# A new order of the work ahead of the MLP: scalings off GpSimd, a token tile loaded ahead of the weight transposes

## The chip, the cores and the metric

The kernel runs on one core of a Trainium2 chip. The metric is the device time of one execution in microseconds; the median of three runs stands for a kernel. The engines are TensorE (PE), VectorE (DVE), ScalarE (ACT), GpSimd (POOL) and SyncE (SP), which here only issues DMAs.

## What is computed

One transformer block over 2048 tokens of width 576, in bfloat16:

```python
def _A_ref(x, wqkv, w_phi, wo):          # 32 heads of 18
    qkv = (x @ wqkv) -> q, k, v per head
    pq, pk = q @ w_phi, k @ w_phi        # per head, 18 x 18
    phi_q = concat(softmax(pq), softmax(-pq)); phi_k = likewise
    kv = sum over tokens of phi_k^T v;  z = sum over tokens of phi_k
    o = (phi_q @ kv) / (phi_q @ z + 1e-6)
    return o @ wo
def _B_ref(x, w1, b1, w2, b2):           # hidden width 4608
    return gelu(layernorm(x) @ w1 + b1) @ w2 + b2
h  = x + _A_ref(layernorm(x), ...)
h2 = h + _B_ref(layernorm(h), ...)
```

The sums over tokens (kv, z) run over all keys, so no query can be finished until every key has been through; then the MLP follows, tile by tile.

## The kernel before

The 2048 tokens are 16 tiles of 128, handled as 8 pairs `p` with halves. The program has two parts. The first takes all keys and values, and the queries' feature maps, and ends with the first token pair normalised for the MLP. The second is the MLP and what is left of the attention output, in blocks of one or two pairs (`first_block` to `double_block`), and it keeps TensorE busy to the end.

The order in the first part is written out by hand: a flat list of calls, lines 772 to 1103. All five engines are under manual scheduling, so each engine executes its own instructions in the order in which the calls issue them, and each DMA queue likewise. A call whose operands are not ready holds up everything behind it on the same engine. The calls:

- `load_x` loads tokens, `load_values` the value weights, `turn_wk` and `turn_wq` transpose the key and query weights from DRAM (three DMA transposes each, on SP's queue); `load_phi` loads w_phi on ScalarE's queue.
- `spread(g)` (GpSimd) lays w_phi out in blocks; `fold_k_mm`/`fold_k_ev` multiply it into the key weights, nine products with a copy out of PSUM each; `fold_mm("q", c)`/`fold_ev` do the same to the query weights in five, and `swap_q` copies parts of them to the other half of the partitions by DMA.
- `stats(p, i)` (VectorE) and `power` (GpSimd's pow) give mean and reciprocal deviation. `scale(p, i, engine)` normalises one tile: a tensor_scalar on VectorE or GpSimd, or an activation on ScalarE, for which `centre` (GpSimd) prepares the shift.
- Pairs 0 and 1 are transposed on TensorE (`turn_x_mm`, `turn_x_ev`), pairs 2 to 7 by DMA (`turn_dma`), which waits for both scaled halves.
- `key_mm`, `value_mm`, `query_mm` are projections, 18 matmuls each. `key_exp`, `query_exp` write two exponentials of each to a buffer, `key_sum`, `query_sum` (VectorE) sum over each head and take reciprocals, `key_weigh`, `query_weigh` multiply by them, on VectorE or GpSimd.
- `sums(p, a)` adds one tile's keys and values up in PSUM; `window_masks` (GpSimd) makes the mask that `table` (VectorE) applies to the finished sums. Then `turn_q`, `combine_mm`, `divide`, `turn_o_mm`, the residual and the second normalisation follow, and `turn2_mm` hands the first tile to the MLP.

Projections, folds and transposes share one PSUM pool, `two`, of three buffers: a fourth waits for the copy or exponential that empties the first. The exponentials of the keys have five buffers for eight pairs. `filler(n)` issues n small matmuls that compute nothing that is used.

Of the kernel before, what the change touches and what calls it, by code (L numbers as in the profile page):

```python
# [45 lines left out]
def kernel(  # L46
# [148 lines left out]
    load_x(1, 2, nc.scalar)  # L195
# [586 lines left out]
    scale(0, 0, vec)  # L782
    spread(3)
    spread(1)
    scale(0, 1, vec)
    spread(2)
    turn_x_mm(0)
    fold_k_mm(7)
    turn_x_ev(0, 0, dve)
    turn_x_ev(0, 1, dve)  # L790
    filler(6)
    fold_k_mm(5)
    stats(1, 0)
    fold_k_ev(7, act)
    fold_k_ev(5, act)
    fold_k_mm(4)
    fold_k_ev(4, act)
    stats(1, 1)
    fold_k_mm(0)
    power(1, vec)  # L800
    stats(3, 0)
    scale(1, 1, pool)
    fold_k_ev(0, act)
    scale(1, 0, vec)
    stats(3, 1)
    load_values(1, syn)
    load_values(2, syn)
    stats(2, 0)
    filler(4)
    fold_k_mm(2)  # L810
    filler(3)
    fold_k_mm(3)
    filler(3)
    fold_k_mm(1)
    fold_k_ev(3, act)
    fold_k_ev(2, act)
    filler(11)
    fold_k_mm(8)
    load_values(3, syn)
    fold_k_ev(1, act)  # L820
    stats(2, 1)
    power(3, pool)
    fold_k_ev(8, act)
    fold_k_mm(6)
    filler(8)
    turn_x_mm(1)
    fold_k_ev(6, act)
    scale(3, 0, vec)
    turn_x_ev(1, 0, act)
    turn_x_ev(1, 1, act)  # L830
    value_mm(0, 1)
    value_ev(0, 1, act)
    key_mm(1, 0)
    power(2, vec)
    load_x(12, 16, syn)
    value_mm(1, 1)
    centre(2, 0)
    key_mm(0, 0)
    stats(6, 0)
    key_exp(1, 0)  # L840
    stats(6, 1)
    scale(2, 0, act)
    load_x(8, 12, syn)
    centre(3, 1)
    scale(2, 1, pool)
    value_mm(0, 0)
    value_ev(1, 1, act)
    key_exp(0, 0)
    power(6, pool)
    turn_dma(2)  # L850
    key_mm(0, 1)
    value_ev(0, 0, act)
    turn_wq(1)
    scale(3, 1, act)
    value_mm(1, 0)
    stats(4, 0)
    stats(4, 1)
    value_mm(2, 0)
    stats(5, 0)
    turn_dma(3)  # L860
    power(4, vec)
    key_exp(0, 1)
    stats(5, 1)
    turn_wq(0)
    power(5, pool)
    centre(4, 1)
    load_b1()
    value_ev(1, 0, act)
    key_mm(2, 1)
    value_ev(2, 0, act)  # L870
    scale(5, 1, pool)
    key_sum(1, 0)
    turn_wq(2)
    scale(4, 1, act)
    key_sum(0, 1)
    key_mm(1, 1)
    scale(6, 0, pool)
    key_weigh(0, 1, 0, pool)
    key_exp(2, 1)
    scale(4, 0, vec)  # L880
    value_mm(3, 1)
    key_weigh(0, 1, 1, vec)
    key_sum(0, 0)
    key_mm(3, 1)
    stats(7, 0)
    key_exp(1, 1)
    scale(5, 0, pool)
    turn_dma(4)
    value_ev(3, 1, act)
    key_sum(1, 1)  # L890
    key_mm(2, 0)
    key_exp(3, 1)
    value_mm(2, 1)
    key_exp(2, 0)
    turn_dma(5)
    key_mm(3, 0)
    value_ev(2, 1, act)
    key_sum(2, 0)
    key_weigh(1, 0, 0, vec)
    key_weigh(0, 0, 1, pool)  # L900
    value_mm(3, 0)
    stats(7, 1)
    key_exp(3, 0)
    key_weigh(0, 0, 0, pool)
    value_ev(3, 0, act)
    key_weigh(1, 0, 1, pool)
    fold_mm("q", 0)
    key_mm(4, 0)
    scale(6, 1, vec)
    fold_ev("q", 0, act)  # L910
    key_weigh(1, 1, 1, pool)
    value_mm(4, 1)
    fold_mm("q", 1)
    sums(0, 0)
    key_exp(4, 0)
    fold_mm("q", 3)
    key_sum(4, 0)
    sums(1, 1)
    key_sum(2, 1)
    value_ev(4, 1, act)  # L920
    fold_ev("q", 1, act)
    load_wo(1)
    fold_ev("q", 3, act)
    fold_mm("q", 4)
    key_weigh(1, 1, 0, pool)
    sums(0, 1)
    fold_mm("q", 2)
    key_weigh(2, 0, 1, pool)
    sums(1, 0)
    window_masks()  # L930
    fold_ev("q", 4, act)
    value_mm(5, 0)
    power(7, pool)
    key_sum(3, 1)
    key_mm(4, 1)
    fold_ev("q", 2, act)
    value_ev(5, 0, act)
    turn_dma(6)
    scale(7, 1, vec)
    key_exp(4, 1)  # L940
    key_mm(5, 0)
    key_exp(5, 0)
    swap_q(0)
    key_mm(5, 1)
    swap_q(1)
    key_weigh(4, 0, 1, vec)
    key_exp(5, 1)
    key_mm(6, 1)
    key_weigh(2, 0, 0, pool)
    key_exp(6, 1)  # L950
    key_sum(5, 0)
    value_mm(5, 1)
    centre(7, 0)
    swap_q(2)
    query_mm(5, 0)
    load_w1(0, 2, syn)
    value_ev(5, 1, act)
    query_mm(0, 1)
    query_exp(5, 0)
    key_sum(3, 0)  # L960
    query_exp(0, 1)
    key_weigh(2, 1, 0, pool)
    key_sum(5, 1)
    key_weigh(5, 0, 1, pool)
    query_mm(3, 0)
    query_mm(0, 0)
    load_w1(0, 0, syn)
    key_sum(6, 1)
    scale(7, 0, act)
    query_exp(3, 0)  # L970
    value_mm(4, 0)
    query_sum(0, 1)
    query_exp(0, 0)
    value_ev(4, 0, act)
    query_mm(4, 0)
    query_exp(4, 0)
    key_mm(6, 0)
    sums(2, 0)
    key_weigh(2, 1, 1, pool)
    key_weigh(6, 1, 0, vec)  # L980
    sums(2, 1)
    turn_dma(7)
    key_exp(6, 0)
    value_mm(6, 1)
    key_weigh(3, 1, 0, pool)
    key_weigh(5, 0, 0, pool)
    query_sum(0, 0)
    key_weigh(3, 0, 1, pool)
    value_ev(6, 1, act)
    key_mm(7, 1)  # L990
    key_sum(6, 0)
    value_mm(6, 0)
    key_sum(4, 1)
    value_mm(7, 1)
    key_exp(7, 1)
    key_sum(7, 1)
    value_ev(6, 0, act)
    key_weigh(3, 0, 0, pool)
    key_mm(7, 0)
    value_ev(7, 1, act)  # L1000
    value_mm(7, 0)
    key_exp(7, 0)
    value_ev(7, 0, act)
    query_mm(7, 0)
    key_weigh(6, 1, 1, pool)
    load_w1(0, 4, syn)
    turn_b1()
    key_weigh(4, 1, 0, vec)
    key_weigh(4, 0, 0, pool)
    key_weigh(3, 1, 1, pool)  # L1010
    key_weigh(5, 1, 0, pool)
    query_weigh(0, 1, 0, vec)
    query_mm(2, 0)
    query_exp(7, 0)
    key_weigh(5, 1, 1, pool)
    load_wo(3)
    query_mm(7, 1)
    key_weigh(6, 0, 1, vec)
    key_sum(7, 0)
    query_weigh(0, 1, 1, pool)  # L1020
    query_weigh(0, 0, 0, pool)
    load_w1(0, 3, syn)
    key_weigh(7, 1, 1, pool)
    key_weigh(6, 0, 0, pool)
    query_weigh(0, 0, 1, pool)
    key_weigh(7, 0, 1, vec)
    query_exp(7, 1)
    key_weigh(4, 1, 1, pool)
    query_mm(6, 0)
    load_wo(0)  # L1030
    sums(3, 0)
    load_w1(0, 1, syn)
    load_wo(2)
    key_weigh(7, 1, 0, vec)
    sums(6, 1)
    query_exp(6, 0)
    sums(5, 0)
    sums(6, 0)
    turn_q(0)
    sums(4, 0)  # L1040
    sums(5, 1)
    query_exp(2, 0)
    key_weigh(7, 0, 0, pool)
    sums(4, 1)
    sums(3, 1)
    sums(7, 1)
    sums(7, 0)
    query_mm(3, 1)
    table(0)
    combine_mm(1, 0, two)  # L1050
    table(1)
    combine_mm(0, 0)
    combine_mm(1, 1)
    combine_mm(0, 1)
    divide(1)
    query_exp(3, 1)
    query_mm(4, 1)
# [232 lines left out]
```

## Time and profile before

| | |
|---|---|
| median of three runs | 395.31 us (394.77 to 396.99) |
| the profiled execution | 395.63 us |
| its span | 393.9 us |
| granted TensorE clock | 1.0 |
| busy time: PE, DVE, ACT, POOL | 381.9, 172.0, 160.3, 122.6 us |

The span is the time from the first to the last instruction in the profile; the execution's time is somewhat longer. A line of the timeline gives start, duration, engine, line of the kernel, operation, output and inputs with their shapes, the number of instructions, and in brackets how long the engine idled before them and what released it. SPq marks DMAs that SP issues. A line of the groups gives the busy time of all, the mean in ns of one, and the idle time before them. A line of the chain gives start, length and what took it.

### The profile page before, as it was taken

The page shows a single profiled execution, that of the slowest core. Times are in us where ns is not written, and L with a number is a line of the kernel's source. Part 1 is how long each engine was busy: PE and PEld are TensorE (multiplying, and loading weights), DVE is VectorE, ACT ScalarE, POOL GpSimd, SP SyncE. Part 2 cuts the span into 40 slices and gives each one's busy share as a digit, 9 for nine tenths or more (in the row PEclk, how much of TensorE's full clock was granted, in tenths as well). Part 3 has the DMA queues.
Part 4 walks back from the last instruction along what each step waited for, and adds up shares of the span by engine and source line. Part 5 has one row for each costly group of instructions (what it writes and reads, how often), then busy time and mean ns, then how long its engine had stood idle before and what let it go on. Part 6 is the DMA issues. An engine that isn't in the chain of part 4 may idle for free.

```text
span 393.9 us, 10162 instructions
## 1 busy us (share of the span) xinstructions
PE 381.9 (97%) x4466; PEld 267.7 (68%) x4467; DVE 172.0 (44%) x370; ACT 160.3 (41%) x287; POOL 122.6 (31%) x151
## 2 busy tenths in 40 slices
PE   7979998899999999999999999999999999999997
PEld 3767876669977887854457887444677764447773
DVE  5898999777139568681009323000380000000100
ACT  2878887378700870036660000566400016661000
POOL 4669899414604554235002211000032110000120
PEclk9999999999999999999999999999999999999999
DMA  8776967999853678333003372000042000000000
GB/s 190 263 109 125 178 137 151 198 274 308 241 106 76 122 105 135 77 77 73 2 2 62 75 120 47 15 2 2 2 93 60 17 15 2 2 2 0 17 27 20
DMA packets 75280, 34.71 MB, mean 88 GB/s; under 512 B 62788, under 2 KB 72708, under 8 KB 75236
## 3 DMA queue, kind: packets, MB, share of 16 engines
q1 hardware_dynamic: 73984, 32.41, 39.2%
q0 software_dynamic: 336, 1.33, 1.3%
q8 instruction: 35, 0.57, 0.6%
q10 hardware_dynamic: 916, 0.32, 0.4%
q14 instruction: 9, 0.07, 0.1%
HBM read 15.81 MB, written 2.36 MB: 46 GB/s over the span
## 4 chain that ended last, share of the span: by engine, by line
PE 78%; POOL 7%; DVE 6%; DMA 4%; issue 1%; ACT 1%; SPq 1%; POOLq 0%; DVEq 0%
PE po L1174 36%; PE ph L1130 36%; POOL phik L490 5%; PE pa L705 4%; DMA xh<-in_A_x_dram 2%; DMA w<-in_A_wqkv_dram 1%; PE pn L656 1%; DVE phik L490 1%; DMA home<-shared 1%; POOL shared L331 1%; DVE st L308 1%; DVE sk L484 1%; PE pk L433 1%; ACT phik L455 1%; POOL padded L519 1%
## 5 line engine op out<-in xcount | busy, mean ns | idle before, releaser
L1152 ACT ACTIVATE home<-ph,b1col 128x512 bf16<-128x512 f32 (+1 forms) x180 | 98.5, 598 | 169.3 <-PE ph L1130 165.9
L1174 PE MATMUL po<-w,home 128*128 128x288 bf16 (+2 forms) x1151 | 143.3, 286 | 0.1
L1130 PE MATMUL ph<-shared,w 64*128 64x512 bf16 (+2 forms) x1638 | 141.5, 332 | 0.0
L1174 PEld LDWEIGHTS <-home 128*128 128x128 bf16 x1152 | 109.3, 98 | 32.2 <-issue 1.8
L1130 PEld LDWEIGHTS <-w 64*128 64x128 bf16 x1638 | 80.4, 94 | 59.9 <-issue 0.7
L1178 DVE TENSOR_TENSOR ot<-po,hb 128x288 bf16<-128x288 f32 (+2 forms) x32 | 14.5, 454 | 106.6 <-PE po L1174 100.7
L1163 POOL TENSOR_TENSOR hb<-xh,b2bc 128x576 f32<-128x576 bf16 x16 | 20.3, 1272 | 104.6 <-DVE ot L1178 104.6
L433 PEld LDWEIGHTS <-home 64*128 64x128 bf16 x864 | 42.5, 94 | 12.6 <-DMA home<-shared 2.6
L519 POOL TENSOR_TENSOR padded<-home,rq 128x540 bf16<-128x540 bf16 x31 | 33.8, 1101 | 36.4 <-DVE rq L511 18.9
L714 DVE TENSOR_TENSOR xh<-pa,xh 128x288 bf16<-128x288 f32 x32 | 13.0, 448 | 71.9 <-PE pa L705 71.9
L270 POOL TENSOR_TENSOR rs<-va,mhalf 128x1 f32<-128x1 f32 x16 | 8.8, 550 | 103.9 <-DVE va L268 103.9
L490 POOL TENSOR_TENSOR phik<-phik,rk 128x576 bf16<-128x576 bf16 x24 | 30.1, 1282 | 3.3 <-DVE rk L486 3.3
L433 PE MATMUL pv<-wv,home 64*128 64x288 bf16 x288 | 20.6, 283 | 2.3 <-DMA home<-shared 2.3
L455 ACT ACTIVATE home<-pk 128x576 bf16<-128x576 f32 x32 | 18.5, 658 | 9.1 <-PE pk L433 9.0
L484 DVE TENSOR_REDUCE sk<-phik 128x64 f32<-128x1152 bf16 x16 | 21.0, 1313 | 1.8 <-ACT phik L455 1.7
L510 DVE TENSOR_REDUCE sk<-home 128x64 f32<-128x1152 bf16 x16 | 21.0, 1312 | 0.0
L455 ACT ACTIVATE phik<-pk 128x576 bf16<-128x576 f32 x32 | 18.8, 662 | 3.5 <-PE pk L433 2.6
L669 DVE RECIPROCAL rec<-pn 128x18 f32<-128x18 f32 (+1 forms) x32 | 8.0, 250 | 27.9 <-PE pn L656 27.9
L433 PE MATMUL pk<-shared,home 64*128 64x288 bf16 x288 | 19.8, 283 | 0.0
L433 PE MATMUL pk<-wqp,home 64*128 64x288 bf16 x288 | 18.8, 283 | 0.0
L705 PE MATMUL pa<-wo,shared 64*128 64x288 bf16 x288 | 18.7, 283 | 0.0
L705 PEld LDWEIGHTS <-shared 64*128 64x128 bf16 x288 | 13.8, 94 | 4.6 <-issue 0.5
(74 smaller groups left out, 218.9 us busy)
## 6 DMA issues: line engine op xcount, KB each, us to landing
w<-in_B_w_dram SPq DMA_DIRECT2D x21, 432.0 KB, 7.1
out_dram<-ot SPq DMA_DIRECT2D x15, 144.0 KB, 2.0
xh<-in_A_x_dram SPq DMA_DIRECT2D x3, 576.0 KB, 7.0
wo<-in_A_wo_dram SPq DMA_DIRECT2D x4, 324.0 KB, 5.3
w<-in_B_w_dram POOLq DMA_DIRECT2D x3, 432.0 KB, 11.6
wv<-in_A_wqkv_dram SPq DMA_DIRECT2D x2, 576.0 KB, 7.7
wqp<-wqp SPq DMA_DIRECT2D x2, 288.0 KB, 3.5
xh<-in_A_x_dram ACTq DMA_DIRECT2D x2, 144.0 KB, 3.2
```

Source lines behind the costliest of these rows:

```text
L433: nc.tensor.matmul(dst[:, a, 0:HALF], lhs[rows, c, :], w[rows, slot, i * HALF : (i + 1) * HALF], start=(n == 0), stop=(n == KC - 1),)
L455: nc.scalar.activation(rows[:, :, i * HH : (i + 1) * HH, s, :], flight[key, p, i][:, :, 0:HALF].rearrange("p a (h f) -> p a h f", f=DH), A ...
L484: nc.vector.tensor_reduce(sk[:, :, :], part_of(dst, i), AX.X, ALU.add)
L490: eng.tensor_tensor(part, part, flight["r" + key, p, i][:, a, :].rearrange("p (h o) -> p h o", o=1).to_broadcast([P, NH, DH]), ALU.mult,)
L510: nc.vector.tensor_reduce(sk[:, :, :], part_of(phiq[p], i), AX.X, ALU.add)
L519: eng.tensor_tensor(padded[:, a, g0 * P : (g0 + 5) * P].rearrange("p (g k) -> p g k", k=P)[:, :, 0:STEP].rearrange("p g (h f) -> p g h f", ...
L705: nc.tensor.matmul(pa[a], oT[p % 2][rows, c, :], wo[rows, c, cs], start=(c == 0), stop=(c == KC - 1),)
L1130: nc.tensor.matmul(ph[half][:, lo:hi], w1[p_ // 9][rows, c, p_ % 9 * P : (p_ % 9 + 1) * P], ln2T[rows, c, base + lo : base + hi], start=(c ...
L1152: nc.scalar.activation(hidden(m), ph[half][:, 0:width], AF.Gelu_apprx_tanh, bias=b1col[:, m : m + 1], scale=1.0,)
L1163: nc.gpsimd.tensor_tensor(hb[:, :], xh[:, t, :], b2bc[:, :], ALU.add)
L1174: nc.tensor.matmul(po[:, :], hidden(m)[:, i_ * P : (i_ + 1) * P], w2[m // 18][:, m % 18, cs], start=(j == 0), stop=(j == NM - 1),)
L1178: nc.vector.tensor_tensor(ot[:, cs], po[:, :], hb[:, cs], ALU.add)
```

## The change

The first part's list is put in a new order, and some calls name another engine. Behind the list, nothing differs. The number of calls of each kind is the same, but for the fillers (35 before, 34 after).

- Scalings: before, seven on VectorE, four on ScalarE, five on GpSimd; after, ten on VectorE, six on ScalarE, none on GpSimd. Two more `centre` calls come with the two on ScalarE.
- Key weighings: before, 24 on GpSimd and eight on VectorE; after, 27 and five. Query weighings of pair 0: before, three on GpSimd and one on VectorE; after, all four on GpSimd.
- The second token tile is loaded on SP's queue, ahead of the three key weight transposes, where ScalarE's queue had it.
- On SP's queue, tokens 8 to 12 now come ahead of 12 to 16; two query weight transposes come ahead of the first token pair's; tokens 12 to 16 come behind that pair's.
- `window_masks` moves from the middle of the list to behind the last key weighing of GpSimd.

The changed lines, first the load, then the start of the new list, then its middle and end in part (a key weighing, query weighing or scaling that stands on VectorE or ScalarE is shown wherever it is; the lines taken out are left away but for the first):

```diff
     load_x(0, 1, nc.scalar)
-    load_x(1, 2, nc.scalar)
+    load_x(1, 2, nc.sync)
     load_phi(nc.scalar)
     for n in range(len(TURNS)):
         turn_wk(n)
...
     warm(18)
+    spread(0)
+    spread(2)
+    stats(0, 0)
     load_x(2, 4, syn)
-    spread(0)
-    stats(0, 0)
+    spread(3)
+    stats(0, 1)
     load_x(4, 8, syn)
+    load_values(1, syn)
     power1(0, 0, vec)
-    stats(0, 1)
     power1(0, 1, vec)
+    scale(0, 1, vec)
+    scale(0, 0, vec)
+    spread(1)
     spread(4)
+    fold_k_mm(2)
+    fold_k_ev(2, dve)
+    stats(1, 0)
+    fold_k_mm(5)
+    fold_k_ev(5, act)
+    fold_k_mm(7)
+    filler(6)
+    fold_k_mm(8)
     load_values(0, syn)
...
+    turn_x_ev(0, 1, act)
...
+    scale(1, 1, vec)
+    scale(1, 0, vec)
+    load_x(8, 12, syn)
...
+    turn_x_mm(1)
+    centre(2, 0)
+    key_mm(0, 0)
     load_values(2, syn)
     turn_x_ev(1, 0, act)
     turn_x_ev(1, 1, act)
+    power(3, pool)
+    key_exp(0, 0)
+    turn_wq(0)
     key_mm(1, 0)
+    centre(3, 0)
+    scale(2, 1, vec)
     scale(2, 0, act)
     value_mm(0, 0)
     stats(4, 0)
     stats(4, 1)
+    stats(5, 0)
+    centre(3, 1)
+    key_exp(1, 0)
+    power(4, vec)
+    scale(3, 1, act)
+    stats(5, 1)
+    value_ev(0, 0, act)
+    turn_wq(2)
+    turn_dma(2)
+    value_mm(1, 1)
+    key_sum(0, 0)
+    load_x(12, 16, syn)
+    value_ev(1, 1, act)
+    centre(4, 0)
+    key_weigh(0, 0, 0, pool)
+    value_mm(1, 0)
+    stats(6, 0)
+    scale(3, 0, act)
...
+    scale(4, 0, act)
...
+    key_weigh(1, 0, 0, pool)
     value_mm(2, 0)
+    centre(5, 1)
+    key_sum(0, 1)
+    scale(4, 1, act)
+    power(6, pool)
+    scale(5, 0, vec)
...
+    turn_dma(4)
+    value_ev(2, 1, act)
+    scale(5, 1, act)
+    key_sum(1, 1)
+    scale(6, 0, vec)
...
+    turn_wq(1)
+    key_sum(2, 1)
+    fold_mm("q", 3)
+    scale(6, 1, vec)
...
+    turn_dma(5)
...
+    turn_dma(6)
...
+    scale(7, 1, vec)
...
+    scale(7, 0, vec)
...
+    key_weigh(4, 1, 0, vec)
...
+    query_weigh(0, 1, 0, pool)
+    query_weigh(0, 1, 1, pool)
...
+    key_weigh(7, 1, 0, vec)
+    value_ev(6, 0, act)
+    load_w1(0, 2, syn)
+    key_weigh(6, 0, 0, vec)
+    turn_q(0)
...
+    key_weigh(3, 0, 1, pool)
+    query_mm(6, 0)
+    key_weigh(7, 0, 1, vec)
+    key_weigh(6, 1, 0, pool)
+    key_weigh(7, 0, 0, vec)
+    key_weigh(7, 1, 1, pool)
     value_mm(7, 1)
+    load_w1(0, 3, syn)
...
+    window_masks()
+    query_exp(2, 0)
     load_wo(2)
...
     sums(7, 0)
+    table(0)
```

More of the change, by code (lines that the diff above doesn't have):

```diff
@@ new lines @@
+    key_weigh(2, 1, 1, pool)
+    sums(0, 1)
+    value_ev(4, 1, act)
+    fold_mm("q", 0)
+    fold_mm("q", 1)
+    turn_dma(5)
+    stats(7, 0)
+    fold_ev("q", 3, act)
+    turn_dma(6)
+    stats(7, 1)
+    sums(0, 0)
+    key_sum(4, 0)
+    fold_mm("q", 2)
+    load_b1()
+    fold_ev("q", 0, act)
+    fold_ev("q", 1, act)
+    power(7, pool)
+    fold_ev("q", 2, act)
+    sums(1, 1)
+    sums(1, 0)
+    fold_mm("q", 4)
+    key_mm(5, 1)
+    value_mm(5, 0)
+    fold_ev("q", 4, act)
+    swap_q(2)
@@ new lines @@
+    key_weigh(3, 0, 0, pool)
+    key_weigh(2, 0, 1, pool)
+    key_weigh(4, 0, 0, pool)
+    key_mm(5, 0)
+    key_exp(5, 1)
+    value_ev(5, 0, act)
+    scale(7, 1, vec)
+    key_exp(5, 0)
+    key_mm(4, 1)
+    swap_q(0)
+    swap_q(1)
+    key_mm(6, 1)
+    load_wo(3)
+    sums(2, 0)
+    key_sum(3, 1)
+    scale(7, 0, vec)
+    sums(2, 1)
+    key_weigh(4, 0, 1, pool)
+    query_mm(0, 1)
+    turn_dma(7)
+    key_weigh(3, 1, 0, pool)
+    key_sum(5, 0)
+    key_exp(4, 1)
+    key_exp(6, 1)
@@ new lines @@
+    key_weigh(3, 1, 1, pool)
+    query_mm(4, 0)
+    key_weigh(5, 0, 1, pool)
+    load_w1(0, 0, syn)
+    query_mm(0, 0)
+    query_exp(0, 1)
+    query_exp(4, 0)
+    key_sum(6, 1)
+    load_w1(0, 4, syn)
+    query_mm(5, 0)
+    query_exp(0, 0)
+    value_mm(6, 1)
+    key_weigh(5, 0, 0, pool)
+    key_sum(5, 1)
+    query_exp(5, 0)
+    value_mm(5, 1)
+    key_weigh(5, 1, 1, pool)
+    key_weigh(5, 1, 0, pool)
+    key_mm(7, 1)
+    load_w1(0, 1, syn)
+    key_sum(4, 1)
+    query_sum(0, 0)
```

376 lines of the change are left out of this document (118 added, 258 removed).

## The prediction

> **What bounds the kernel now.** I read the windows view by stage first, then the timeline around each gap of TensorE, then the groups by line for prices. Its columns: window, length, then busy time (instructions) of PE, PEld, DVE, ACT, POOL, granted clock, DMA share, GB/s.
>
> ```profile
> span 393.9 us, 10162 instructions
> 8.00:15.20 7.20, 6.24 (x104) 5.52 (x105) 5.96 (x19) 5.22 (x10) 4.11 (x6) 1.00 1.05 343
> 15.20:23.00 7.80, 7.80 (x128) 6.95 (x126) 6.75 (x24) 6.90 (x12) 5.24 (x8) 1.00 0.59 117
> 23.00:25.60 2.60, 0.31 (x7) 0.04 (x4) 2.53 (x5) 1.26 (x3) 1.33 (x4) 1.00 0.66 135
> 25.60:67.20 41.60, 41.60 (x703) 33.10 (x703) 39.12 (x48) 33.80 (x59) 38.38 (x36) 1.00 0.80 153
> 67.20:73.80 6.60, 4.05 (x114) 3.55 (x114) 5.96 (x7) 2.40 (x5) 4.50 (x4) 1.00 0.92 128
> 73.80:88.00 14.20, 13.09 (x213) 9.74 (x211) 10.04 (x30) 9.44 (x18) 3.22 (x5) 1.00 1.05 254
> ...
> 88.03 18.02 PE ph L1130 x342
> ```
>
> The MLP starts at 88.0 (last line, from the chain), and from there TensorE has no gap worth naming. The code behind that point is untouched, so the change is worth what it moves this start. Ahead of it TensorE idles in two places: 2.3 us between 23.0 and 25.6, and 2.5 us in 67.2 to 73.8. In between it is busy 41.60 of 41.60 us, while DVE and POOL are busy 39.1 and 38.4: all three are full, and the end of the stage shows who is late:
>
> ```profile
> 15.20 1.46 PE L433 MATMUL pv<-wv,home 64*128 64x288 bf16 x18
> 20.45 1.33 SPq L338 DMA_TRANSPOSE home<-shared  x1
> 25.57 1.28 PE L433 MATMUL pv<-wv,home 64*128 64x288 bf16 x18 [2.29 <-DMA home<-shared]
> 42.03 4.57 PE L433 MATMUL pk<-shared,home 64*128 64x288 bf16 x72
> ...
> 63.96 0.69 DVE L490 TENSOR_TENSOR phik<-phik,rk 128x576 bf16<-128x576 bf16 x1
> 69.00 2.37 PE L569 MATMUL acc_kv<-vals,phik 128*128 128x57 bf16 x77 [1.30 <-DVE phik L490]
> 70.97 2.39 DVE L490 TENSOR_TENSOR phik<-phik,rk 128x576 bf16<-128x576 bf16 x2
> 73.79 0.50 DVE L582 TENSOR_TENSOR kvm<-acc_kv,wmask 128x324 bf16<-128x324 f32 x1 [0.43 <-PE acc_kv L569]
> ```
>
> The first gap is the DMA transpose of token pair 2 (issued 20.45, used 25.57: 5.1 us). The second is the weighing: the sums over the keys (seven calls in 2.37, so 0.34 each) wait for VectorE, whose last weighings end at 73.36; the table that closes the stage starts at 73.79. I call that time T. One projection costs 1.10 (four in 4.57, the last tail taken off).
>
> **The change part by part.** Prices:
>
> ```profile
> L331 POOL TENSOR_SCALAR shared<-xh,mv,rs 128x576 bf16<-128x576 bf16 x5 | 11.4, 2285 | 1.6 <-POOL nb L280 1.0 <-DVE phik L490 0.5
> L331 DVE TENSOR_SCALAR shared<-xh,mv,rs 128x576 bf16<-128x576 bf16 x7 | 3.6, 522 | 0.3 <-POOL rs L317 0.3
> L490 POOL TENSOR_TENSOR phik<-phik,rk 128x576 bf16<-128x576 bf16 x24 | 30.1, 1282 | 3.3 <-DVE rk L486 3.3
> L490 DVE TENSOR_TENSOR phik<-phik,rk 128x576 bf16<-128x576 bf16 x8 | 9.6, 1216 | 0.1
> L519 DVE TENSOR_TENSOR padded<-home,rq 128x540 bf16<-128x540 bf16 x1 | 1.7, 1674 | 0.0
> L529 DVE TENSOR_TENSOR padded<-home,rq 128x72 bf16<-128x72 bf16 x1 | 1.2, 1187 | 0.0
> L484 DVE TENSOR_REDUCE sk<-phik 128x64 f32<-128x1152 bf16 x16 | 21.0, 1313 | 1.8 <-ACT phik L455 1.7
> L486 DVE RECIPROCAL rk<-sk 128x64 f32<-128x64 f32 x16 | 8.8, 553 | 0.7
> L308 DVE BATCH_NORM_STATS2 st<-xh 128x6 f32<-128x288 bf16 x32 | 12.6, 434 | 1.6 <-DMA xh<-in_A_x_dram 1.4
> ```
>
> *Who does what.* Counted in the diff: all five scalings leave GpSimd (11.4 us), three go to VectorE (3 x 0.52) and two to ScalarE. The few words say all weighings go to GpSimd; the diff leaves five key weighings on VectorE. What moves is three key weighings (3 x 1.22 off VectorE, 3 x 1.28 onto GpSimd) and one query weighing (1.67 + 1.19 off VectorE).
>
> *The opening.*
>
> ```profile
> 0.79 4.64 SPq L158 DMA_TRANSPOSE w<-in_A_wqkv_dram  x3
> 0.79 0.87 ACTq L186 DMA_DIRECT2D xh<-in_A_x_dram  x2
> 9.01 5.10 ACT L395 CAST shared<-pW 128x576 bf16<-128x576 f32 x9 [3.85 <-PE pW L388]
> ```
>
> The second token tile now stands ahead of the three weight transposes on SP's queue: one issue, 0.87/2 = 0.43 us, by which they start later; the three loads of w_phi behind it on ScalarE's queue go 0.43 earlier. Folding (the nine casts, 0.57 each) waits for the transposes, so it starts 0.4 later; one cast goes to VectorE, one transpose copy comes to ScalarE in its stead, so the row of nine is no shorter. Bounds 0 to 1.0 for the first projection (15.20 now); I take 0.5, at 15.7, as the nearest row is the one issue.
>
> *Pair 2's transpose.* Its ScalarE half now stands behind one projection and one exponential pair:
>
> ```profile
> 26.89 0.64 ACT L443 CAST vals<-pv 128x576 bf16<-128x576 f32 x1 [2.62 <-PE pv L433]
> 27.42 0.87 ACT L286 ACTIVATE shared<-xh,nb,rs 128x576 bf16<-128x576 bf16 x1
> 28.19 2.27 ACT L455 ACTIVATE phik<-pk 128x576 bf16<-128x576 f32 x4
> ```
>
> Starts lie 0.53 (value), 0.77 (scaling) and 1.1 (pair of exponentials) apart. 15.7 + 1.25 + 1.1 + 0.9 = 19.0 for the issue, where it was 20.45; the VectorE half stands behind the stats of pairs 1 to 3, which before are done, one set apart, when VectorE takes up tokens 12 to 16 at 17.6 (9.34 + 8.26, below); with one cast and three scalings more and two copies' half less I take 17.9, between 17.0 and 19.0. Landing 5.1 later, 24.1. TensorE's seven projections before it end at 15.7 + 7.7 = 23.4, so the gap shrinks from 2.3 to under 1 and the eighth starts near 24.2, 1.4 earlier than 25.57. ScalarE has six scalings instead of three ahead of the 18th projection: 9 x 1.1 + 9 x 0.53 + 6 x 0.77 = 19.3 against 18 x 1.10 = 19.8 of TensorE, so they are covered by 0.5 us; beyond that each would hold a PSUM buffer.
>
> *TensorE's path.* Between the eighth projection and the ten last sums stands the same work as before (67.2 - 25.57 = 41.6). The transposes of the query weights' middle part and of pair 6 come just as they are needed: 0 to 2 us, I take 0.8. 24.2 + 41.6 + 0.8 = 66.6, ten sums 3.4: T no earlier than 70.0.
>
> *VectorE's path.* This is where a new wait arises. Tokens 12 to 16 are loaded behind pair 2's transpose, not ahead of it:
>
> ```profile
> 9.34 8.26 DMA xh<-in_A_x_dram
> xh<-in_A_x_dram SPq DMA_DIRECT2D x3, 576.0 KB, 7.0
> xh<-in_A_x_dram SPq DMA_DIRECT2D x1, 288.0 KB, 3.5
> ```
>
> Issue at about 20.4, ready by 20.9; landing 3.5 to 8.26 later, at L = 24.4 to 29.2. I take 5.5 (L = 26.4): the long rows fell in the windows at 343 GB/s, this one falls where 117 to 135 are moved, but shares them with transposes. Stats of pair 6 stand on VectorE behind four stats (about 1.0 each with their aggregate) and one key sum (1.3 + 0.55): 17.9 + 3.9 + 1.8 = 23.6. So VectorE stalls 2.8. Queued behind the waiting stats on VectorE are the key sum of pair 1 and all later ones; GpSimd's next weighing waits for that sum, and behind this weighing stands the shift for pair 5's scaling, for which ScalarE waits. That shift comes at L + 1.0 + 1.85 + 1.28 + 0.3 (the shift itself, an estimate between nothing and the 0.52 of a scaling of full width) = 30.8; ScalarE reaches the scaling at 17.0 + 5 x 1.1 + 6 x 0.53 + 5 x 0.77 = 29.5. It loses 1.3, and the three PSUM buffers pass on between nothing and all of that to TensorE, 70.0 to 71.3; I take the half, 70.6. VectorE's own end: from 17.6 on, before has the same stats and sums ahead of it and ends at 73.36. So: 73.4 + 0.3 (start) - 3.7 (three weighings) - 2.9 (query weighing) + 1.0 (two scalings more from there on) - 1.7 (its waits for exponentials, which a later VectorE no longer has) + 2.8 (stall) + 1.0 (two of the four last weighings run beside GpSimd's, at 2.39 - 0.69 = 1.7, not 1.2) = 70.2.
>
> *GpSimd's path.* Its last four weighings start at the sum of pair 6, which ends one sum (1.85) and four weighings (4.8) before that, at 63.6; two at 1.28 and two at 1.7 end at 69.6. The masks that the table needs now come after them:
>
> ```profile
> 41.34 0.12 POOL L236 MEMSET full<- 128x33 f32 x1
> 42.41 0.19 POOL L248 TENSOR_SCALAR_AFFINE_SELECT wmask<-low 128x3 f32<-128x3 f32 x1
> ```
>
> 1.26 us from first to last: 70.9, T = 71.0. So GpSimd with its masks ends last, VectorE 0.5 before it (70.2, and 0.3 for the last sum), TensorE 0.4: the three are nearly level, and a us lost on any of them moves T by most of a us. T goes from 73.8 to 71.0: 2.8 us.
>
> *Behind T.* The order there changes little: the same seven projections, residual adds and statistics. The combination needs the transposed queries:
>
> ```profile
> 67.51 3.11 SPq L555 DMA_TRANSPOSE shared<-padded  x2
> 74.89 0.80 PE L656 MATMUL pn<-kvm,shared 128*128 128x57 bf16 x22
> ```
>
> 7.4 us from issue to use; GpSimd has weighed the queries by 63.6, so 71.0, under T + 1.1 for the projection between. Cover 1.1 us; if it is gone, every further us counts. Behind that transpose on SP now stand one part of the first w1 quarter, one part of wo and the bias transpose, where before there was one part of w1 and b2. wo's part is wanted by the first residual product, which stands behind four projections, so at T + 4.4 = 75.4 or later; issued by 63.6 + 3.1 + 1.2 = 67.9, it has 7.5 us, enough for the 7.0 of the loads above; a landing of 8.26 would cost 0.8 at most. 88.0 - 73.8 = 14.2 stays.
>
> *The sum.* Span 393.9 - 2.8 = 391.1; the profiled execution took 395.63, so 392.8. The median of the three runs is 395.31: 392.5.
>
> **A rule against the change.**
>
> ```profile
> 43.65 1.16 POOL L490 TENSOR_TENSOR phik<-phik,rk 128x576 bf16<-128x576 bf16 x1
> 43.97 0.47 DVE L331 TENSOR_SCALAR shared<-xh,mv,rs 128x576 bf16<-128x576 bf16 x1
> ```
>
> A VectorE scaling inside a GpSimd weighing: 1.16, below the mean of 1.28, so neither paid. The Trainium skill ("SBUF — State Buffer", section "Who interferes with whom") says that a VectorE tensor_scalar can enter a mode that takes the port pair shared with GpSimd, and that the second to start then waits for the whole instruction; this row does not show it for this scaling.
>
> **The rivals.**
> 1. *The late tokens cost all that is won.* L = 29.2, the longest landing seen: T = L + 44.6 = 73.8, 395.3. For it: that row; against it: DMA is half as loaded at 21 us. 0.16.
> 2. *Scalings hold up GpSimd.* Five scalings of VectorE fall among weighings; at 0.52 each GpSimd ends 2.6 later: T = 73.6, 395.1. The rows just shown speak against it. 0.06. This is what the skill's page would make of the time.
> 3. *Slower: SP's queue.* Two of the three query weight transposes now stand ahead of pair 2's; before, none did. If they keep it from issuing (the DMA is at 1.05 of its engines' time until 15.2), each us goes to the stall and to TensorE's gap. Issue at 22.5, tokens ready to move at 24.4, landing 7.0 later at 31.4: T = 76.0, 397.5. It decides from L = 29.2 on. For it: ScalarE waits too, since pair 5's shift stands on GpSimd behind a weighing that waits for the same stats; against it: 6 us lie between those issues and the scaling. 0.16.
>
> **How the numbers follow.** This kernel's measurement can tell about 0.5% (2.0 us) from no change. Forecast, with T from 69.3 (TensorE without its 0.8) to 71.8: 0.62, faster. Rivals 1 and 2 lie within 0.5%: 0.22. Rival 3: 0.16. The forecast's own range is 390.5 to 393.3. The whole range goes from 390.2 to 396.6, which takes in rivals 1 and 2 and the near half of rival 3.
>
> **What would show it.** Right: first projection near 15.7; pair 2's transpose issued near 19.0 and TensorE waiting under 1 us for it; VectorE idle for tokens near 23.6 by 1 to 5 us; the table near 71.0, released by the masks; the MLP near 85.2. Wrong: GpSimd weighings lengthened by scalings, an SP issue of pair 2 later than 20.5, or a wait for the transposed queries behind T. The forecast fails if the table starts after 71.8.

## The result and the profile after

The kernel with the change takes 391.96 us (median of five runs, 391.37 to 392.87) against 395.31 us for the kernel before, measured beside it: a ratio of 0.991 [0.9881, 0.9939]. Ranges and ratios are of the fast executions; two far slower ones, of 2268.42 us in a run below and of 665.81 us for the kernel before beside another, are left out. The profiled execution took 391.96 us. The first line of its page, and the start of the MLP in its chain of waits:

```profile
span 390.3 us, 10160 instructions
84.35 18.02 PE ph L1130 x342
```

The MLP starts at 84.35 instead of 88.03, so all of the gain lies ahead of it. The windows view over the same stretches as before (length, then busy time of PE, PEld, DVE, ACT, POOL, granted clock, DMA share, GB/s):

```profile
15.20:23.00 7.80, 7.80 (x127) 6.29 (x127) 7.56 (x24) 7.34 (x13) 3.52 (x9) 1.00 1.19 162
23.00:25.60 2.60, 2.60 (x48) 2.42 (x44) 0.87 (x2) 2.60 (x6) 1.47 (x3) 1.00 1.15 186
25.60:67.20 41.60, 41.27 (x728) 34.41 (x725) 40.58 (x55) 34.42 (x61) 37.07 (x38) 1.00 0.80 155
67.20:73.80 6.60, 5.90 (x133) 4.78 (x131) 5.18 (x12) 3.08 (x6) 5.13 (x10) 1.00 0.80 177
```

TensorE's first gap is gone (2.60 busy of 2.60 where it was 0.31), and the second is 0.7 us where it was 2.5. The timeline of the same kernel shows the places that the prediction named (start, duration, engine, line, operation, operands, count, in brackets the idle time before and its releaser):

```profile
8.78 2.27 ACT L395 CAST shared<-pW 128x576 bf16<-128x576 f32 x4 [4.25 <-PE pW L388]
10.79 0.82 DVE L308 BATCH_NORM_STATS2 st<-xh 128x6 f32<-128x288 bf16 x2 [1.52 <-DMA xh<-in_A_x_dram]
...
15.69 2.38 PE L433 MATMUL pk<-shared,home 64*128 64x288 bf16 x36
18.98 1.30 SPq L338 DMA_TRANSPOSE home<-shared  x1
20.33 0.59 SPq L186 DMA_DIRECT2D xh<-in_A_x_dram  x1
22.47 3.49 PE L433 MATMUL pk<-shared,home 64*128 64x288 bf16 x54
25.83 0.82 DVE L308 BATCH_NORM_STATS2 st<-xh 128x6 f32<-128x288 bf16 x2 [1.93 <-DMA xh<-in_A_x_dram]
30.29 0.87 ACT L286 ACTIVATE shared<-xh,nb,rs 128x576 bf16<-128x576 bf16 x1 [0.75 <-POOL nb L280]
...
33.80 7.91 POOL L490 TENSOR_TENSOR phik<-phik,rk 128x576 bf16<-128x576 bf16 x7
37.73 0.48 DVE L331 TENSOR_SCALAR shared<-xh,mv,rs 128x576 bf16<-128x576 bf16 x1
...
62.86 6.07 POOL L490 TENSOR_TENSOR phik<-phik,rk 128x576 bf16<-128x576 bf16 x4
63.21 6.33 DVE L490 TENSOR_TENSOR phik<-phik,rk 128x576 bf16<-128x576 bf16 x4
68.98 1.10 PE L569 MATMUL acc_kv<-vals,phik 128*128 128x57 bf16 x28 [0.70 <-POOL phik L490]
69.77 0.29 POOL L248 TENSOR_SCALAR_AFFINE_SELECT wmask<-low 128x30 f32<-128x30 f32 x1
70.19 0.50 DVE L582 TENSOR_TENSOR kvm<-acc_kv,wmask 128x324 bf16<-128x324 f32 x1 [0.65 <-PE acc_kv L569]
71.22 0.80 PE L656 MATMUL pn<-kvm,shared 128*128 128x57 bf16 x22
```

The table starts at T = 70.19, 3.60 earlier than before. Where that comes from can be added up with one window from the first projection to the table in each kernel, before and then after:

```profile
15.20:73.79 58.59, 53.75 (x943) 43.64 (x943) 54.36 (x81) 44.37 (x77) 49.46 (x50) 1.00 0.78 145
```

```profile
15.69:70.19 54.50, 53.47 (x945) 44.70 (x945) 50.87 (x81) 45.43 (x79) 44.90 (x54) 1.00 0.88 161
```

TensorE's idle time falls from 4.84 to 1.03 us (3.81 won), its busy time by 0.28, and the first projection starts 0.49 later: together 3.60. Behind T, the way to the MLP is as long as before (84.35 - 70.19 = 14.2; before 88.03 - 73.79 = 14.2). The time of the profiled execution less T is 321.8 us in both kernels and in seven of the eleven runs below: T belongs to that one execution, and the median can differ from it.

### The profile page after: what moved, and what is told of

It is laid out like the page before. It is cut to its first block, busy times and chain, and to the rows that moved or that the text cites. A ratio compares the mean times of both kernels' runs of the same rounds, so it can differ in the third digit from the quotient of the medians.

```text
span 390.3 us, 10160 instructions
## 1 busy us (share of the span) xinstructions
PE 381.9 (98%) x4465; PEld 268.7 (69%) x4466; DVE 167.7 (43%) x366; ACT 161.5 (41%) x289; POOL 115.8 (30%) x155
## 3 DMA queue, kind: packets, MB, share of 16 engines
q0 software_dynamic: 336, 1.33, 1.4%
## 4 chain that ended last, share of the span: by engine, by line
PE 82%; DVE 6%; POOL 5%; DMA 3%; issue 1%; SPq 1%; ACT 1%; ACTq 0%; POOLq 0%
PE po L1174 36%; PE ph L1130 36%; PE pa L705 4%; POOL phik L490 3%; DMA xh<-in_A_x_dram 3%; PE pk L433 2%; DVE sk L484 2%; PE pn L656 1%; DVE st L308 1%; SPq L158 1%; POOL padded L519 1%; ACT phik L455 1%; DVE shared L331 1%; DVE rk L486 1%; PE pv L433 1%
## 5 line engine op out<-in xcount | busy, mean ns | idle before, releaser
L1163 POOL TENSOR_TENSOR hb<-xh,b2bc 128x576 f32<-128x576 bf16 x16 | 20.4, 1274 | 104.6 <-DVE ot L1178 102.8
L433 PEld LDWEIGHTS <-home 64*128 64x128 bf16 x864 | 43.5, 94 | 9.9 <-issue 1.1
L519 POOL TENSOR_TENSOR padded<-home,rq 128x540 bf16<-128x540 bf16 x32 | 35.2, 1113 | 38.1 <-DVE rq L511 19.6
L490 POOL TENSOR_TENSOR phik<-phik,rk 128x576 bf16<-128x576 bf16 x27 | 32.1, 1226 | 4.3 <-DVE rk L486 4.3
L433 PE MATMUL pv<-wv,home 64*128 64x288 bf16 x288 | 19.3, 283 | 0.3 <-ACT vals L443 0.3
```

Of the source, the lines that this page charges most:

```text
L433: nc.tensor.matmul(dst[:, a, 0:HALF], lhs[rows, c, :], w[rows, slot, i * HALF : (i + 1) * HALF], start=(n == 0), stop=(n == KC - 1),)
L490: eng.tensor_tensor(part, part, flight["r" + key, p, i][:, a, :].rearrange("p (h o) -> p h o", o=1).to_broadcast([P, NH, DH]), ALU.mult,)
L519: eng.tensor_tensor(padded[:, a, g0 * P : (g0 + 5) * P].rearrange("p (g k) -> p g k", k=P)[:, :, 0:STEP].rearrange("p g (h f) -> p g h f", ...
L1163: nc.gpsimd.tensor_tensor(hb[:, :], xh[:, t, :], b2bc[:, :], ALU.add)
```

## The experiments

Two questions were open after the result: what the two prices cost, the late tokens and the late first projection, and which part brings the gain. The theory at first was that the new share of the engines carries most of it, as the terms of the forecast have it; the rivals were that the new order does, or that each is needed for the other. T is the start of the table in the profiled execution of every run; ratios are against the kernel before. T contains a difference between executions: in four kernels whose opening is the same but for a load that comes later (the change, two runs that move weighings, and one that moves tokens 12 to 16), the first projection starts at 15.69, 15.66, 15.56 and 15.22. Where a run leaves the opening alone, the stretch from the first projection to T, 54.50 with the change, is the better measure. Edits are shown against the kernel with the change unless said otherwise.

**The late tokens: much earlier.** Tokens 12 to 16 are loaded right behind tokens 8 to 12:

```diff
     load_x(8, 12, syn)
+    load_x(12, 16, syn)
     stats(2, 1)
...
     key_sum(0, 0)
-    load_x(12, 16, syn)
     value_ev(1, 1, act)
```

> The changed kernel, with tokens 12 to 16 loaded right behind tokens 8 to 12, ahead of pair 2's transpose. Theory of three level paths: VectorE's 1.9 us idle at 23.9 goes, VectorE and GpSimd end their last weighings 1.5 to 1.9 earlier, and then TensorE alone sets the end of the sums (last projection 65.5, ten sums 3.4): the table starts at 69.2 to 69.6 instead of 70.2, the time falls by 0.6 to 1.0 us. Rival, TensorE or the transposed queries set it already: no change. Rival, the earlier 576 KB hold up the value weights: the first value projection (17.9) slips and the time rises by 0.5 or more.

Measured: 390.85 us, 0.9872 [0.985, 0.9895], T = 69.27. Its timeline:

```profile
19.96 3.61 PE L433 MATMUL pv<-wv,home 64*128 64x288 bf16 x56 [1.62 <-DMA wv<-in_A_wqkv_dram]
65.83 3.33 PE L569 MATMUL acc_kv<-vals,phik 128*128 128x57 bf16 x110
69.27 0.50 DVE L582 TENSOR_TENSOR kvm<-acc_kv,wmask 128x324 bf16<-128x324 f32 x1 [1.22 <-PE acc_kv L569]
```

The stall for tokens went, and the ten last sums (110 matmuls) run in one piece. But the load now stands ahead of two blocks of value weights, and TensorE waits 1.62 us for those. The first projection stands at 14.98 here, and from it to T it takes 54.29 us instead of 54.50: behind the opening, the new wait took nearly all that the old one gave back.

**The late tokens: the place between.** The same load stands behind the value weights and ahead of the first query weight transpose:

```diff
     load_values(2, syn)
+    load_x(12, 16, syn)
     turn_x_ev(1, 0, act)
...
     key_sum(0, 0)
-    load_x(12, 16, syn)
     value_ev(1, 1, act)
```

> The changed kernel with tokens 12 to 16 loaded behind the last value weights and ahead of the query weight transposes. Theory that the late tokens cost VectorE 1.9 us and that the run with the tokens earlier gave part of it back to the value weights (TensorE waited 1.6 for them): no wait for value weights, VectorE's wait for tokens under 1 us, table at 68.3 to 69.3, time 390.0 to 391.0 us. Rival, the last weighings set the end whatever comes earlier: table at 69.2 to 69.6 as there, no gain over it.

Measured: 390.8 us, 0.9878 [0.9863, 0.9893], T = 68.54, in the expected band. The timeline has no wait for value weights or tokens, and the end of the stage is one piece:

```profile
65.11 3.32 PE L569 MATMUL acc_kv<-vals,phik 128*128 128x57 bf16 x110
68.54 0.50 DVE L582 TENSOR_TENSOR kvm<-acc_kv,wmask 128x324 bf16<-128x324 f32 x1 [1.39 <-PE acc_kv L569]
```

T is 1.65 earlier than in the kernel with the change, but 0.47 of this is the opening: the first projection stands at 15.22, and the difference is there before the moved load is issued at 10.43 (VectorE takes up the second pair's tokens at 10.32, with the change at 10.79). From the first projection to T it takes 53.32 us, 1.18 less, and by the medians the time is 1.2 us shorter: this is what the late tokens cost. The two intervals overlap a little, but all four executions (390.34 to 391.13) lie below the five with the change (391.37 to 392.87). Between the two early places the medians are level (390.85 and 390.8); the profiled executions (391.03 and 390.34) differ by as much as T does.

**The scalings alone, taken back.** The five scalings return to GpSimd, everything else stays:

```diff
-    scale(1, 1, vec)
+    scale(1, 1, pool)
...      # likewise (2, 1), (5, 0), (6, 0)
-    centre(5, 1)
-    scale(5, 1, act)
+    scale(5, 1, pool)
```

> The changed kernel in its new order, with the five scalings that were on GpSimd put back there (one shift less). Theory that GpSimd's load counts: tile 3's scaling delays the second transpose on TensorE by about 1.1 us (first projection 16.8), and three scalings of 2.3 us in the weighing stage, less the idle time that GpSimd has there, put its last weighing 3 to 5 us later: table at 74 to 76, time 396 to 398 us, slower than before. Rival, only VectorE's relief from weighings counts: the table moves by the opening's 1.1 alone, time about 393.

Measured: 400.93 us, 1.0133 [1.0106, 1.016], T = 77.85: slower than the kernel before, and by more than expected. Its timeline:

```profile
20.73 1.30 SPq L338 DMA_TRANSPOSE home<-shared  x1
27.77 0.82 DVE L308 BATCH_NORM_STATS2 st<-xh 128x6 f32<-128x288 bf16 x2 [4.95 <-DMA xh<-in_A_x_dram]
44.37 0.70 PE L569 MATMUL acc_kv<-vals,phik 128*128 128x57 bf16 x11 [7.07 <-POOL phik L490]
```

The first projection stands at 16.23, 0.54 later than with the change, and the scaling of pair 2 on GpSimd delays that pair's transpose further, from 18.98 to 20.73, and the tokens queued behind it on SP, so VectorE waits 4.95 for them instead of 1.93; then TensorE waits 7.07 for a weighing of GpSimd. Behind this wait its granted clock is 0.50 (from 44.40 to 47.00), so the wait costs more than its length.

**The scalings taken back, with the tokens early.** This tells GpSimd's load from the queue on SP: the edit above together with the place between for tokens 12 to 16.

```diff
     load_values(2, syn)
+    load_x(12, 16, syn)
...
-    scale(1, 1, vec)
+    scale(1, 1, pool)
...      # the other four as above
```

> The run with the five scalings put back on GpSimd, now with tokens 12 to 16 ahead of the query weight transposes. What is open there is why it cost 9 us where 3 to 5 had been expected. Theory that the late scaling of pair 2 held up its transpose and the tokens behind it on SP's queue, so that VectorE waited 5.0 us for them: the wait goes, the table is at 73 to 75 instead of 77.8, time 395.5 to 397.5 us. Rival, GpSimd's three scalings ahead of the weighings of the first sums account for it: VectorE's wait goes, but the table stays at 77 or later, time 400 us.

Measured: 395.0 us (394.11 to 395.30), 0.9982 [0.9965, 1.0], T = 72.7: both a little below the expected bands, and VectorE's wait for tokens is gone. Against 390.8 with the same tokens, the scalings on GpSimd cost 4.2 us. Against 400.93, the earlier tokens bring 5.9, where they bring 1.2 when VectorE scales. So the miss of the run above was a coupling: a late scaling makes the transpose late, and the tokens behind it in the queue. A part of the 5.9 is the lower clock behind the long wait, which is missing here (TensorE's longest wait for a weighing is 1.84 us, and the clock stays at 1.00).

**The weighings alone, taken back.**

```diff
-    key_weigh(1, 0, 0, pool)
+    key_weigh(1, 0, 0, vec)
...      # likewise (0,1,1), (4,0,1), (6,0,1), (6,1,0) and query_weigh(0, 1, 0)
-    key_weigh(6, 0, 0, vec)
+    key_weigh(6, 0, 0, pool)
...      # likewise (7,0,0)
```

> The changed kernel in its new order, with the weighings on the engines they had before (eight key weighings and one query weighing on VectorE). Theory that VectorE is one of three level paths: 3.7 + 2.9 us come back to it, table at 74.5 to 76.5, time 396 to 398 us. Rival, TensorE's earlier start is what won: table at 70 to 71.5, time 392 to 393.

Measured: 396.06 us, 1.0 [0.9985, 1.0016], T = 74.55, at the lower end of what was expected. The end of the stage in its timeline:

```profile
62.57 1.27 DVE L519 TENSOR_TENSOR padded<-home,rq 128x540 bf16<-128x540 bf16 x1
63.77 1.13 DVE L529 TENSOR_TENSOR padded<-home,rq 128x72 bf16<-128x72 bf16 x1
68.53 5.21 DVE L490 TENSOR_TENSOR phik<-phik,rk 128x576 bf16<-128x576 bf16 x4
73.11 1.33 PE L569 MATMUL acc_kv<-vals,phik 128*128 128x57 bf16 x33 [0.89 <-DVE phik L490]
```

VectorE ends last again, as before the change, at 73.74. Three of the key weighings given back to it stand ahead of its query sums, and the first of its last two query sums starts 3.0 us later than with the change (56.51 against 53.49); the query weighing adds 2.3 ahead of its last key sums. The new order with this share of the weighings is worth nothing.

**Order and engines apart.** The kernel before with the new engines alone, then the new order with the engines of before (the five scalings and the eight weighings both taken back, as in the two runs above). The edit of the first:

```diff
     # the order of before, with the engines of the change
-    scale(1, 1, pool)
+    scale(1, 1, vec)
...
-    key_weigh(0, 1, 1, vec)
+    key_weigh(0, 1, 1, pool)
...      # all 16 calls that name another engine (8 scalings, 8 weighings), and the centre calls
```

> The kernel before in its old order and with its old loads, every scaling and weighing on the engine it has in the changed kernel (the shifts for ScalarE placed just ahead of their scalings). Theory that the engines carry the change: the weighings no longer end last, TensorE's gap ahead of pair 2 stays at 2 us or more, table at 70.3 to 71.5, time 392 to 393 us. Rival, the order carries it: table at 73 or later, time 394.5 or more.

Measured: 401.88 us, 1.0159 [1.0131, 1.0188], T = 78.6. The theory that the share of the engines carries the gain falls. The windows and the timeline of this kernel show what happened:

```profile
40.00:55.00 15.00, 15.00 (x267) 12.18 (x265) 13.40 (x17) 13.18 (x24) 6.65 (x7) 1.00 0.56 120
```

```profile
49.13 2.28 POOL L490 TENSOR_TENSOR phik<-phik,rk 128x576 bf16<-128x576 bf16 x2 [3.91 <-DVE rk L486]
54.53 10.14 POOL L490 TENSOR_TENSOR phik<-phik,rk 128x576 bf16<-128x576 bf16 x9 [3.12 <-PE pv L433]
76.55 2.00 PE L569 MATMUL acc_kv<-vals,phik 128*128 128x57 bf16 x39 [5.34 <-POOL phik L490]
```

GpSimd, freed of the scalings, stands idle for more than half of 40 to 55 (6.65 busy of 15), since its next weighings wait for sums that come later in that order (1.33 and 3.91 us) and then, by the profile, for a projection (3.12 us), and then it is full to the end: TensorE waits 5.34 us for its last weighings.

> The changed kernel's order and loads, every scaling and weighing on the engine it had before: the fourth corner beside before, changed and the run with the engines alone. Theory that order and engines only pay together: GpSimd's scalings stand ahead of its first weighings and TensorE waits at the first sums as in the run with the scalings put back, VectorE is loaded too; table at 77 to 80, time 400 to 404 us. Rival, the two parts add up (engines alone cost 6.3, together they win 3.4): the order alone would win 9.7 us, 386 us.

Measured: 401.09 us, 1.0142 [1.0126, 1.0157], T = 79.1, as expected. This corner is not exact, other than the text ahead of it says: the scalings of two tiles that the change moves from VectorE to ScalarE, and of one that it moves back, stay where the change has them. With that, the engines alone cost 1.6% and the order nearly alone 1.4%, and both together win 0.9%: they pay only together.

**The new engines in the old order, with GpSimd's own queue sorted.** In the kernel with the new engines in the old order, each of GpSimd's 27 key weighings now stands right behind the key sum that it needs:

```diff
     # against the order of before with the new engines
+    key_weigh(1, 0, 0, pool)
+    key_weigh(1, 0, 1, pool)
...
-    key_weigh(1, 0, 0, pool)
-    key_weigh(0, 0, 1, pool)
...
```

> The run with the engines alone in the old order, with one thing changed: each of GpSimd's 27 key weighings stands right behind the sum that it waits for. What is open is why the engines alone cost 6 us. Theory that GpSimd's old queue is what fails: it idles from 44 to 54 us behind weighings whose sums come late, and then has too much left; sorted, the idle time goes, the table is at 70.5 to 73 instead of 78.6, time 392 to 395 us. Rival, the rest of the old order (the sums on VectorE, pair 2's late transpose) keeps it there: table at 76 or later, time 399 us or more.

Measured: 410.72 us, 1.0392 [1.0357, 1.0426], with T = 74.3. T moved 4.3 the right way, to between the bands of theory and rival, but the time was missed widely. Timeline and windows:

```profile
72.46 2.67 POOL L519 TENSOR_TENSOR padded<-home,rq 128x540 bf16<-128x540 bf16 x2
88.51 1.21 PE L656 MATMUL pn<-kvm,shared 128*128 128x57 bf16 x22 [13.03 <-DMA shared<-padded]
```

```profile
80.00:88.00 8.00, 0.00 (x0) 0.00 (x0) 0.00 (x0) 0.00 (x0) 0.00 (x0) 0.50 1.12 163
88.00:100.00 12.00, 11.46 (x163) 8.43 (x165) 6.34 (x20) 5.26 (x10) 0.36 (x1) 0.81 1.06 238
```

The sorted key weighings pushed pair 0's query weighings to the end of GpSimd's queue. Their transposes, issued at 74.10, then ran beside loads of the MLP's weights, with the DMA at 1.12 of its engines' time, and TensorE idled 13 us. GpSimd's order explains 4.3 of the 8.4 us by which T of the old order with the new engines lies behind that of the change. The rest, with VectorE's order of sums and the pairs' transposes as candidates, stays open.

**The last weighings on VectorE.** Three of the four last key weighings of GpSimd go to VectorE:

```diff
-    key_weigh(3, 0, 1, pool)
+    key_weigh(3, 0, 1, vec)
...      # likewise (6, 1, 0) and (7, 1, 1)
```

> The changed kernel with GpSimd's last three key weighings on VectorE, which then has seven of the last eight. Theory that the two engines hold each other up there (1.58 us each beside each other, 0.70 alone on VectorE): seven weighings take 1.6 + 6 x 0.65 = 5.5 us from 63.2, against 6.3 for four now; table at 69.0 to 69.6 instead of 70.2, time 0.6 to 1.2 us less. Rival, 1.58 is what these weighings cost VectorE anyway: 11 us, table at 75, time 4 to 5 us more.

Measured: 391.31 us, 0.9898 [0.9881, 0.9916], T = 69.53, in the expected band. The timeline:

```profile
62.59 1.16 POOL L490 TENSOR_TENSOR phik<-phik,rk 128x576 bf16<-128x576 bf16 x1
62.94 5.46 DVE L490 TENSOR_TENSOR phik<-phik,rk 128x576 bf16<-128x576 bf16 x7
```

VectorE does seven in 5.46 us, nearly alone, where it did four in 6.33 beside GpSimd's four. T moves 0.66 (0.13 of it in the opening), the time by less than the two intervals can tell.

**The second token tile on ScalarE's queue again.**

```diff
-    load_x(1, 2, nc.sync)
+    load_x(1, 2, nc.scalar)
```

> The changed kernel with the second token tile loaded on ScalarE's queue as before. Theory that the one issue on SP's queue delays what stands behind it by 0.4 us: the three key weight transposes and tokens 2 to 4 start 0.4 earlier, the first projection at 15.2 to 15.5 instead of 15.7, the time falls by 0 to 0.4 us. Rival, w_phi's later loading then holds the folding up by as much: first projection at 15.7 or later, no change.

Measured: 391.3 us, 0.989 [0.9876, 0.9905], T = 69.5:

```profile
15.09 2.38 PE L433 MATMUL pk<-shared,home 64*128 64x288 bf16 x36
```

The first projection comes 0.60 earlier, a little more than expected, and T 0.7; from the one to the other it takes 54.4, as with the change. But executions with one and the same opening differ by 0.5 there, and the time is shorter by less than the intervals can tell: this run alone does not show that the new place of the load costs. The next one does.

**The two together.** Tokens 12 to 16 in the place between, and the second token tile on ScalarE's queue:

```diff
-    load_x(1, 2, nc.sync)
+    load_x(1, 2, nc.scalar)
...
     load_values(2, syn)
+    load_x(12, 16, syn)
...
-    load_x(12, 16, syn)
```

> The changed kernel with both loads moved: tokens 12 to 16 ahead of the query weight transposes, and the second token tile on ScalarE's queue. Theory that with the tokens early TensorE's own queue sets the end of the sums (ten sums without a gap, as in that run), so that an earlier opening counts in full: first projection at 14.6 to 15.2, table at 67.8 to 68.2, time 0.4 to 0.6 us below the run with the tokens moved alone (390.8). Rival, VectorE or GpSimd end the sums there: table at 68.5, no gain over it.

Measured: 389.21 us (389.02 to 389.47), 0.9838 [0.9812, 0.9863], T = 67.41. It beats both kernels: its interval lies wholly below that of the change. Against the tokens alone it is 1.6 us faster by the medians and 1.1 by the profiled executions, where 0.4 to 0.6 was expected, and all its executions lie below all of that run: the second token tile on SP's queue costs. First projection and T are earlier than expected.

```profile
14.29 2.38 PE L433 MATMUL pk<-shared,home 64*128 64x288 bf16 x36
63.98 3.33 PE L569 MATMUL acc_kv<-vals,phik 128*128 128x57 bf16 x110
67.41 0.50 DVE L582 TENSOR_TENSOR kvm<-acc_kv,wmask 128x324 bf16<-128x324 f32 x1 [1.22 <-PE acc_kv L569]
```

The excess sits at the start: the first projection stands at 14.29, 0.8 earlier than with the token tile's queue alone, although the opening is the same. The traces say where, and not why: the three key weight transposes ahead of the tokens on SP's queue took 4.31 us against 4.70, and VectorE takes up the second pair's tokens at 9.41 against 10.20. From the first projection to T, TensorE is idle for 0.3 us, as the window between the two shows:

```profile
14.29:67.41 53.12, 52.83 (x945) 44.04 (x945) 50.84 (x80) 45.60 (x79) 45.09 (x55) 1.00 0.92 167
```

In this order, little but TensorE's own work is left between the first projection and the table.

## Why the prediction was right, point by point

The forecast was 392.5 us with a T of 71.0. Measured: 391.96 and 70.19. Its rivals 1 and 3 did not come about, and rival 2 is refuted by rows: GpSimd's seven weighings from 33.80 on took 1.13 each although a VectorE scaling of 0.48 lies inside them at 37.73, and the ten from 42.92 on took 1.13 each (11.26 together) with two more scalings inside. A slip without consequence: T = 69.3 gives 390.8 us by the forecast's own sum, and not the 390.5 of its range.

- *The opening.* First projection forecast at 15.7, measured at 15.69. The agreement is luck, and the path was another. The forecast let the folding set it, started 0.4 later; the casts of the folding started at 8.78, where they had started at 9.01. Before the change, TensorE's transposes ahead of the first projection waited for GpSimd's scaling:

```profile
14.59 0.68 PE L355 MATMUL pT<-ident,shared 128*128 128x128 bf16 x9 [0.96 <-POOL shared L331]
```

The change takes this scaling off GpSimd, and in the two runs of the old order with the new engines the first projection came at 14.09 and 14.40 instead of 15.20: a gain that the forecast left out. With the change, the chain of waits goes from the second pair's tokens (VectorE waits 1.52 for them, to 10.79), behind the three weight transposes on SP, over VectorE's statistics and scaling to the first projection. The one issue that the forecast charged does lie on this chain, but its size is open: 0.60 by one pair of runs and 0.93 by the other, with 0.5 between executions of one opening.
- *Pair 2's transpose.* Issue forecast at 19.0, measured at 18.98. TensorE's wait was to shrink to under 1 us; it vanished. The seven projections end, and the eighth starts, at 22.47 + 1.1 = 23.6 where 24.2 was forecast, so the landing took at most 4.6 us, where the forecast carried over 5.1. VectorE's half was scaled at 17.76, forecast at 17.9.
- *The late tokens.* Issue forecast at 20.4, landing at 26.4, stall 2.8. Measured: 20.33, 25.83, 1.93. The landing decided between the forecast and rival 1 (29.2). The forecast argued from a half-loaded DMA (0.59 and 0.66 of its engines' time before); it was at 1.19 and 1.15, and the load took 5.5 us all the same, so the size was right and its reason was not. ScalarE's wait for pair 5's shift was forecast at 1.3 and was 0.75, and of that TensorE lost little: its only gap near there is this one.

```profile
31.73 1.28 PE L433 MATMUL pv<-wv,home 64*128 64x288 bf16 x18 [0.26 <-ACT vals L443]
```

- *What the tokens cost T.* The forecast put the stall into VectorE's end in full. That held: with the tokens in the place between, VectorE's last weighing ends 51.9 us behind the first projection instead of 53.85, 1.9 earlier for a stall of 1.93. T gained only 1.18 of this, since TensorE's own work then ends last.
- *The three paths.* TensorE forecast at 70.6, VectorE's end at 70.2, GpSimd's last weighing at 69.6, then the masks to 70.9. Measured: the sums on TensorE to 70.1 (68.98 + 1.10), VectorE at 63.21 + 6.33 = 69.54, GpSimd at 62.86 + 6.07 = 68.93, the masks of the table's first part at 69.77 + 0.29 = 70.06. They are as level as was said. The step that failed is the order: the profile puts the table's wait down to the sums, not to the masks, though the two end within 0.1 us of each other. The forecast let only two of the four last weighings of each engine run at the higher price of 1.7, 6.0 us for GpSimd's four and 5.8 for VectorE's; all eight ran beside each other and took 6.07 and 6.33. Whether the masks alone would have held T there was not tried. The chain of waits does not pass the table: it goes from GpSimd's last weighing over the sums to the projection behind them.
- *Behind T.* 14.2 forecast, 14.2 measured; the transposed queries were issued at 61.60 and caused no wait. The run that broke this cover (query weighings last on GpSimd) cost 13 us there: each us counted, as forecast, but there were many more of them than the 7.4 us from issue to use before would make one expect.
- *What the argument did not see.* The forecast took the parts as terms that add. Either half alone is slower than before, by 1.4 and 1.6%. The sum came out because both halves were in it and each path was followed to its end, and because what the forecast left out of the opening cancelled; for the engines alone, where 392 to 393 us had been expected, the time was missed by some 9 us.

## What to carry to other kernels

In a program of in-order queues, taking work off an engine pays only if its queue has something ready to put in the room. Change the order and the shares together and follow each engine to its last instruction, since half of such a change can cost more than the whole wins. A load whose data is wanted late still needs a place that does not stand behind a DMA that waits for compute: that one line was worth 1.2 us here, and 5.9, with what the lower clock added, where the compute ahead of it was late.

## What the runs showed of the hardware

The granted TensorE clock dropped within the waits of over 5 us. In the old order with the new engines, TensorE stopped at 71.2 and went on at 76.55:

```profile
73.80:76.00 2.20, 0.00 (x0) 0.00 (x0) 0.00 (x0) 0.00 (x0) 2.20 (x3) 0.61 0.79 147
76.00:79.00 3.00, 2.45 (x45) 2.21 (x47) 0.41 (x1) 0.00 (x0) 0.49 (x1) 0.50 0.87 151
79.00:82.00 3.00, 3.00 (x45) 1.96 (x43) 1.02 (x6) 1.13 (x2) 2.06 (x3) 0.65 0.99 226
82.00:85.00 3.00, 2.64 (x45) 1.90 (x41) 2.20 (x7) 1.26 (x3) 0.00 (x0) 1.00 1.04 224
```

If the clock goes in one step between full and half, a mean of 0.61 puts the drop at 74.3, 3.1 us into the wait, and a mean of 0.65 puts the return at 81.1, 4.5 us after work went on. Windows of half a microsecond agree: 1.00 up to 74.0 and 0.50 from 74.5 on. The same reading of three more runs gives a drop 3.1 us (scalings taken back), 4.8 (order alone) and 3.4 us (GpSimd's queue sorted) into waits of 7.07, 6.36 and 13.03 us, and a return 2.9, 5.3 and 4.0 us after work went on. In the old order with the new engines, the stretch from T to the MLP took 15.4 us instead of 14.2. The wait of 2.29 us in the kernel before left the clock at 1.00. The Trainium skill ("TensorE: Matmul & The Clock Gate", the section on the clock gate in Part 1) gives about 3.4 us of idle time for the drop to half and about as much busy time for the return; here the drop came after 3.1 to 4.8 us and the return after 2.9 to 5.3, so the figures give the size, and single cases lie up to 2 us off them.

Key weighings beside each other cost 1.52 us on GpSimd and 1.58 on VectorE; nearly alone, as in the run with the last weighings on VectorE, they took 1.16 and 0.78 (5.46 / 7). Eight of them, four on each engine, ran from 62.86 to 69.54, 6.7 us, and with seven on VectorE from 62.59 to 68.40, 5.8 us. The Trainium skill ("SBUF — State Buffer", section "Who interferes with whom") says that a VectorE instruction with two SBUF inputs contends with a GpSimd instruction that reads SBUF, and the traces agree.

The two transposes of pair 0's queries took 4.8 us from issue to landing in the kernel before and 3.6 with the change (medians of the two). Where more loads of the MLP's weights ran beside them it was 12.8 us, and 14.4 us passed from the first issue (74.10) to the use (88.51). That the loads are the cause was not tried apart:

```profile
74.10 3.64 SPq L555 DMA_TRANSPOSE shared<-padded  x2
```
